# Order of the MLP outputs, roots and loads at the start of the MLP in a fused attention and MLP kernel

## The chip, the cores and the metric

The kernel runs on one core of a Trainium2 chip. The metric is the device time of one execution in microseconds, smaller is better; the time before is the median of four runs. Five engines work side by side, each through its own list of instructions in the order in which the program wrote them: TensorE (PE: matmuls, and PEld, the loading of weights), VectorE (DVE), ScalarE (ACT), GpSimd (POOL) and SyncE (SP), which here only issues transfers. POOL and, at the start, ACT issue transfers too. An instruction that waits holds back all that stands behind it on its engine.

## What is computed

Attention over 8 batches, 12 heads, 448 positions and 64 columns, with queries and keys normalized by their root mean square, then an MLP over all 3584 positions (768 columns, 2048 hidden).

```python
def rmsnorm(x, g):
    rms = np.sqrt(np.mean(x * x, axis=-1, keepdims=True) + 1e-06)
    return x / rms * g
q_n, k_n = (rmsnorm(q, g_q), rmsnorm(k, g_k))
scores = scale * np.matmul(q_n, k_n.transpose(0, 1, 3, 2))
...
attn = attn / (np.sum(attn, axis=-1, keepdims=True) + 1e-09)
return np.matmul(attn, v).astype(np.float32)
...
x = np.ascontiguousarray(attn_out.transpose(0, 2, 1, 3)).reshape(B * S, H * D)
...
h = x @ w_in
g = np.maximum(h, 0.0) + alpha * np.minimum(h, 0.0)
return (g @ w_out).astype(np.float32)
```

## The kernel before

**Groups.** A batch is cut into three groups of four heads, so there are 24 groups; group `y` belongs to batch `y // 3`. For q and for k of a group, these steps run one after the other:

- `load_qk` (line 97): two transfers each for q and k from HBM into a tile `nat`, four in all, issued by SP. There are six `nat` tiles, so group `y` uses those of group `y - 3`, and can be loaded when that one has been scaled.
- `square` (141): POOL squares `nat` into `sq` (ACT does so for groups 0 and 1). `reduce` (151): VectorE sums the squares over 64 columns into `ss`.
- `root` (159): ACT computes the inverse root by a logarithm and an exponential, for q and k together. `scale` (168): POOL multiplies (`qs`), but for four tiles that VectorE takes.
- The turn to columns-first: groups 0 to 5 are turned on TensorE (`turn`, 188, tiles `tps`). From group 6 on, `turn_dma` (178) lets SP issue two transposing transfers, `qT` and `kT`, as soon as `scale` is done, and `turn` then only has VectorE multiply `kT` by the gain (line 192).

**Attention of a group.** `score` (225) makes one of seven tiles of scores in PSUM (`sc`, two tiles of two banks), `soft` (243) takes the exponential on ACT. `den` (269) sums the exponentials by matmul, `log` and `invert` (276, 281) make the inverse on ACT, `attv` (285) multiplies with the values (`load_v`, 111, issued by POOL) and VectorE writes `xT` (lines 310 and 312).

**MLP.** `up(b, ft)` (344) makes 128 of the 2048 hidden columns of a batch, here called unit `ft`: six matmuls into a PSUM tile, then ACT makes `ah`, which is alpha times that, and VectorE the maximum of both, `gT`. `down` (357) multiplies with `w_out`, VectorE copies the result to `osb` (line 377), and SP issues two stores. The jobs that `down` is handed (reduces of later groups) go ahead of the copy on VectorE, and a `turn` behind it. The PSUM tiles for MLP results are two of one bank each (tag "mm"), and now and then the two-bank tile of tag "acc", which `den` and `attv` use as well. For batch 0, units 0 to 3 begin before the last group of the batch is done (`begin`, 335), and units 2 and 3 share the two banks of one "acc" tile, `hTb`.

**Weights.** `load_w_in` and `load_w_out` (119, 131) are issued by POOL, a quarter at a time. The first half of an output takes quarters 0 and 1 of `w_out`, the second half quarters 2 and 3.

**Order.** The work is put in 69 steps called bursts, each with up to four score tiles. Lines 402 to 485 work out in which burst each step stands: `den_at`, `av_at`, `turn_at`, and from them `prep` (ahead of a burst's scores), `post` (behind all its work), `roots` and `jobs` (steps that go one by one behind the MLP units of the burst). `gaps` holds the MLP units of each burst. A list `late` holds steps that wait until so many units are done. Worked out for the bursts in question:

| burst | score tiles (group, tile) | attention | MLP | other steps |
|---|---|---|---|---|
| 10 | (3,0) (3,1) (3,2) | sums and values of group 2 | units 0 to 4 of batch 0 | root and scale of 4, reduces of 5; behind it, quarters 0 and 1 of `w_out`, squares of 6 |
| 11 | (3,3) (3,4) | | units 5, 6 | root and scale of 5 |
| 12 | (3,5) (3,6) | | units 7, 8 | loads of 7, values of batch 1, turn of 4, quarter 2 of `w_out` |
| 13 | (4,0) (4,1) | | units 9 to 11 | reduces of 6 |
| 14 | (4,2) (4,3) | | units 12, 13 | root, scale and transposes of 6, squares of 7, quarter 3 of `w_out` |
| 15 | (4,4) (4,5) | | units 14, 15 | loads of 8, turn of 5 |
| 16 | (4,6) (5,0) | | one `down` | loads of 9, reduces of 7 |
| 17 | (5,1) (5,2) (5,3) | sums of 3 and 4 | one `down` | root, scale and transposes of 7, turn of 6, squares of 8 |
| 18 | (5,4) (5,5) (5,6) (6,0) | values of 3 and 4 | one `down` | squares of 9 |
| 19 | (6,1) (6,2) (6,3) | sums of 5 | one `down` (second half) | loads of 10, reduces of 8, turn of 7 |
| 20 | (6,4) (6,5) (6,6) | values of 5 | one `down` (second half) | values of batch 2, root, scale and transposes of 8, reduces of 9 |
| 21 | (7,0) (7,1) | | units 0 to 3 of batch 1 | root, scale and transposes of 9 |

Burst 10 is the one that the code calls `lead`: its root and scales wait in `late` until four units are done, and its jobs begin behind the fourth unit (line 704).

Of the kernel before, what the change touches and what calls it, by code (L numbers as in the profile page):

```python
# [10 lines left out]
FP16 = mybir.dt.float16  # L11
AF = mybir.ActivationFunctionType
# [9 lines left out]
def kernel(  # L22
# [12 lines left out]
    nc = tc.nc  # L35

    B, H, S, D = q.shape
# [4 lines left out]
    G = HH // 2  # L42
# [14 lines left out]
    ffn = ctx.enter_context(tc.tile_pool(name="ffn", bufs=2))  # L57
# [26 lines left out]
    alpha_sb = cols[:, :NF]  # L84
# [3 lines left out]
    gT = cst.tile([128, NF, W], FP16, name="gT", tag="gT")  # L88
# [180 lines left out]
    def den(ys):  # L269
        dn = psa.tile([128, 2, 512], FP32, name="dn", tag="acc")  # L270
        over_keys(
            (dn[:, 0], dn[:, 1]), ys, lambda g, y, par, c, j: ones[ds(64 * g, 64), c]
        )
        rden[ys] = dn
# [40 lines left out]
    def bank(name, spare):  # L315
        if spare:
            t = psa.tile([128, 2, 512], FP32, name=name + "a", tag="acc")
            return t[:, 0]
        return psf.tile([128, 512], FP32, name=name, tag="mm")
# [3 lines left out]
    def up_part(hT, b, ft, lo, hi):  # L323

        for i in range(lo, hi):
            for g in range(2):
                nc.tensor.matmul(  # L327
                    out=hT[:, :S],
                    lhsT=w_in_sb[:, g * G + i, ts(ft, 128)],
                    rhs=xT[b][:, g, i, :],  # L330
                    start=(i == 0 and g == 0),
                    stop=(i == G - 1 and g == 1),
                )

    def begin(ft):

        if ft < 2:
            begun[ft] = bank("hT", False)
        elif ft == 2:
            t = psa.tile([128, 2, 512], FP32, name="hTb", tag="acc")  # L340
            begun[2], begun[3] = t[:, 0], t[:, 1]
        up_part(begun[ft], 0, ft, 0, G - 1)

    def up(b, ft, spare=False):
        if b == 0 and ft in begun:
            hT = begun[ft]

            for n in {2: (2, 3), 3: ()}.get(ft, (ft,)):
                up_part(begun[n], 0, n, G - 1, G)
        else:  # L350
            hT = bank("hT", spare)
            up_part(hT, b, ft, 0, G)
        ah = ffn.tile([128, S], FP16, name="ah", tag="ah", bufs=3)
        nc.scalar.activation(out=ah, in_=hT[:, :S], func=AF.Copy, scale=alpha_sb[:, ft : ft + 1])  # L354
        nc.vector.tensor_max(out=gT[:, ft, ds((b & 1) * S, S)], in0=hT[:, :S], in1=ah)  # L355

    def down(b0, t, oh, jobs=(), spare=False):

# [44 lines left out]
    den_at, av_at, split = {}, {}, {}  # L403
# [5 lines left out]
    while m < NG * J or steps:  # L409
        n = len(bursts)  # L410
        while steps:
# [14 lines left out]
        late = both or n in dens and n in avs or any(  # L426
            y >= G for y in dens.get(n, avs.get(n, ()))
        )
        limit = 2 + late + (both and avs[n][0] >= G)
        bursts.append([])  # L430
        while len(bursts[n]) < limit and m < NG * J:
            y, j = divmod(m, J)
# [13 lines left out]
    def at(n, f, *a):  # L446
        prep.setdefault(max(int(n), 0), []).append((f, a))

    def after(n, f, *a):
        post.setdefault(max(int(n), 0), []).append((f, a))  # L450
# [8 lines left out]
    jobs = {}  # L459
    for y in range(G, NG):  # L460

        early = y < G + 2
        if early:
            n = turn_at[y - 1] + 1
        elif y == G + 2:
            n = den_at[G - 1]
        elif y == 2 * G:
            n = turn_at[y] - 4
        elif y % G == 1:
            n = den_at[y - 4] - 1  # L470
        elif y % G:
            n = den_at[y - G]
        else:
            n = av_at[y - 4]
        at(n - (6 if early else 4 if y <= 3 * G else 5), load_qk, y)
        for nm in "qk":
            if y != 2 * G:
                after(n - 2, square, y, nm)
            if early:
                after(n, reduce, y, nm)  # L480
            else:
                jobs.setdefault(n, []).append((reduce, (y, nm)))
        roots[n + 1] = y
    for b in range(1, B):
        at(av_at[G * b] - 6, load_v, b)
# [82 lines left out]
    for n, g in enumerate((g_q, g_k)):  # L568
        for h in range(2):
            nc.gpsimd.dma_start(  # L570
                out=rows[NF + n : NF + n + 1, ds(64 * h, 64)], in_=g.unsqueeze(0)
# [13 lines left out]
    for nm in "qk":  # L585
# [3 lines left out]
        out=gain, in0=cols[:, NF : NF + 1], in1=cols[:, NF + 1 : NF + 2]  # L589
# [25 lines left out]
    for n in range(NB):  # L615
        for f, a in prep.get(n, ()):
            f(*a)
        tiles = bursts[n]

        lead = n == den_at[G - 1]  # L620
        first_tiles = tiles[: 2 if lead else split.get(n, 2)]
        for t in first_tiles:
            score(*t)
            if n == den_at[G - 1] - 1 and t == tiles[-1]:
                begin(0)
                begin(1)
            elif lead and t == tiles[0]:
                soft(*t)
                den(dens[n])
                attv(avs[n], 0, True, (log, invert))  # L630
            elif lead and t == tiles[1]:
                begin(2)
        plain = lead or n not in dens and n not in avs
        wait = plain and not lead and gaps[n] and gaps[n][0][0] is up
        if lead:
            begin(3)
        for t in tiles[:1] if wait else tiles[1:2] if lead else first_tiles:
            soft(*t)
        if n in dens and not lead:
            den(dens[n])  # L640
        if n in avs and not lead:

            for half in (1, 0) if avs[n] == (0, 1) else (0,):
                attv(avs[n], half)
        for t in () if lead else tiles[len(first_tiles) : 3]:
            score(*t)
            soft(*t)
        if n in avs and len(avs[n]) == 2 and avs[n] != (0, 1):
            attv(avs[n], 1)
        for t in () if lead else tiles[max(len(first_tiles), 3) :]:  # L650
            score(*t)
            soft(*t)
        late = []
        if wait:
            late = [(1, soft, t) for t in tiles[1:]]
        if n in roots:
            y = roots[n]
            work = [(root, (y,)), (scale, (y, "q")), (scale, (y, "k"))]
            if lead:

                late = [(2, score, tiles[2]), (2, soft, tiles[2])]
            if lead or wait and y < TD:
                late += [(4 if lead else 1, f, a) for f, a in work]
            else:
                for f, a in work:
                    f(*a)
            if y >= TD:
                turn_dma(y)
        if n in dens and not lead:
            log(dens[n])  # L670
            if gaps[n] and gaps[n][0][0] is down:
                invert(dens[n])
            else:
                late = [(1, invert, (dens[n],))]
        done = 0

        spare_at, clock = [], 0.0
        taken = n + 1 in dens or n + 1 in avs or turns.get(n + 1, TD) < TD
        for k, (f, a) in enumerate(gaps[n]):
            free = 2.3 if n in dens else (0.1, 1.2, 0.0)[len(avs.get(n, ()))]  # L680
            since += 1
            if clock >= free and not turns.get(n, TD) < TD and (
                since > 2 and not (taken and k == len(gaps[n]) - 1) or free == 0.0 and k == 0
            ):
                spare_at.append(k)
                since = 0
            clock += DOWN if f is down else UP
        ups_first = gaps[n] and gaps[n][0][0] is up
        if ups_first and n in dens and not lead:
            for f, a in jobs.pop(n, ()):  # L690
                f(*a)
        turned = n in turns and gaps[n] and (turns[n] >= TD or turns[n] < 2 * G)
        if turned and not ups_first and turns[n] >= TD:
            jobs.setdefault(n, []).append((turn, (turns[n],)))
        elif turned:
            turn(turns[n])
        for k, (f, a) in enumerate(gaps[n]):
            spare = k in spare_at
            if f is down:
                down(*a, jobs.pop(n, ()), spare)  # L700
            else:
                f(*a, spare)
                done += 1
                if n in jobs and not (lead and done < 4):
                    g, c = jobs[n].pop(0)
                    g(*c)
                    if not jobs[n]:
                        del jobs[n]
                while late and done == late[0][0]:
                    _, g, c = late.pop(0)  # L710
                    g(*c)
        if not gaps[n] and n in turns:
            turn(turns[n])
        for _, g, c in late:
            g(*c)
        if n < den_at[G - 1] - 1 and plain and n not in turns:
            spin(1)
        for f, a in jobs.pop(n, []) + post.get(n, []):
            f(*a)
# [32 lines left out]
```

## Time and profile before

| what | us |
|---|---|
| median of 4 runs | 432.69 |
| lowest and highest of them | 432.17, 434.82 |
| profiled execution, whole | 434.8 |
| profiled execution, span | 433.0 |
| TensorE busy in the span | 416.0 |
| idle time of TensorE up to 96 us, and from there on | 12.7, 4.4 |

The profile was taken in one execution with a span of 433.0 us; all times of instructions are in us from the start of that span. The page has the busy time of each engine, the span in 40 slices, the transfers, the chain of work that ended last, and the costliest groups of instructions. Behind it stand views of the same trace: the waits (who waited for whom: total, times, longest), the timeline of an engine (start, length, engine, line, operation, what it writes and reads, how many, and in brackets the idle time before it and what ended it), and the transfers. L355 is line 355 of the code before. Ends of matmuls are modelled, so neighbouring matmuls overlap by some 0.1 us in the timeline.

The granted TensorE clock is 1.00 throughout. The 16 transfer engines are busy for nearly the whole of the first 95 us (8 or 9 tenths in most of those slices) and 0.45 of the time after 140 us.

Units of burst 10 to 12 by the timelines: the matmuls of unit 4 start at 44.77, those of unit 5 at 46.51, of unit 6 at 49.56, of units 7 and 8 at 52.08. The scores of burst 13 start at 54.44, those of burst 17 at 69.60, of burst 21 at 93.56, and the first unit of batch 1 at 94.06.

### The profile page before, as it was taken

How to read it: one execution, taken by the hardware profiler on the slowest of the kernel's cores; microseconds unless marked ns; L12 is line 12 of the kernel's file. 1: busy time of each engine (PE TensorE's matmuls, PEld its weight loads, DVE VectorE, ACT ScalarE, POOL GpSimd, SP SyncE). 2: the span in 40 equal slices, each digit the busy share in tenths (PEclk: the TensorE clock that was granted, in tenths of full speed). 3: DMA queues.
4: the chain of work that ended last, by engine and by line, in shares of the span. 5: the costliest groups of instructions: out<-in, count | busy, mean ns of one | idle time of the engine just before them, and what ended most of it. 6: DMA issues, size and time to landing. Idle time of an engine off the chain costs nothing.

```text
span 433.0 us, 11487 instructions
## 1 busy us (share of the span) xinstructions
PE 416.0 (96%) x4964; PEld 215.9 (50%) x4964; DVE 203.4 (47%) x304; ACT 278.6 (64%) x385; POOL 175.2 (40%) x133
## 2 busy tenths in 40 slices
PE   7789899899999999999999999999999999999996
PEld 3344344444455445544555445554555445555554
DVE  2755664355555363545454463555453353233421
ACT  4997888668876577758757577757757577132300
POOL 4799696384093506380183606471063000000000
PEclk9999999999999999999999999999999999999999
DMA  8999899999759743788059842775074300211133
GB/s 188 232 226 216 149 213 152 224 190 192 169 98 193 166 104 62 156 154 189 21 87 193 170 130 55 147 153 123 20 121 84 77 1 21 56 38 31 25 73 75
DMA packets 70388, 53.85 MB, mean 124 GB/s; under 512 B 37425, under 2 KB 70337, under 8 KB 70337
## 3 DMA queue, kind: packets, MB, share of 16 engines
q1 hardware_dynamic: 55536, 40.19, 43.2%
q0 software_dynamic: 13984, 11.81, 18.9%
q10 hardware_dynamic: 816, 1.11, 1.1%
q8 instruction: 39, 0.64, 0.6%
q14 instruction: 13, 0.10, 0.1%
HBM read 45.62 MB, written 11.01 MB: 131 GB/s over the span
## 4 chain that ended last, share of the span: by engine, by line
PE 83%; DMA 6%; ACT 5%; DVE 4%; issue 1%; POOL 1%; SPq 0%; ACTq 0%
PE op L365 27%; PE hT L327 21%; PE hTa L327 10%; PE sc L232 7%; PE opa L365 6%; DMA w_out_sb<-in_moe_w_out_dram 4%; PE av L261 4%; PE dn L261 4%; ACT expT L246 3%; PE avb L261 2%; DMA nat<-in_k_dram 1%; DVE ss L154 1%; PE tps L206 1%; DVE gT L355 1%; POOL sq L148 1%
## 5 line engine op out<-in xcount | busy, mean ns | idle before, releaser
L246 ACT ACTIVATE expT<-sc,expb 128x896 f16<-128x896 f32 x168 | 161.4, 1003 | 37.9 <-PE sc L232 37.0
L171 POOL TENSOR_TENSOR qs<-nat,rr 128x896 f16<-128x896 f32 x44 | 76.7, 1762 | 149.4 <-issue 79.0
L365 PE MATMUL op<-w_out_sb,gT 128*128 128x384 f16 (+1 forms) x752 | 126.5, 323 | 1.1 <-DMA w_out_sb<-in_moe_w_out_dram 1.1
L365 PEld LDWEIGHTS <-gT 128*128 128x128 f16 x912 | 85.8, 98 | 66.7 <-issue 14.1
L327 PEld LDWEIGHTS <-w_in_sb 128*128 128x128 f16 x768 | 73.2, 98 | 75.9 <-issue 11.6
L327 PE MATMUL hT<-xT,w_in_sb 128*128 128x448 f16 x510 | 107.1, 353 | 2.9 <-DVE gT L355 2.2
L354 ACT ACTIVATE ah<-hT,cols 128x448 f16<-128x448 f32 x85 | 53.7, 633 | 44.6 <-PE hT L327 44.6
L148 POOL TENSOR_TENSOR sq<-nat 128x896 f32<-128x896 f32 x44 | 72.9, 1677 | 9.7 <-DMA nat<-in_q_dram 5.0
L355 DVE TENSOR_TENSOR gT<-hT,ah 128x448 f16<-128x448 f32 x85 | 52.8, 623 | 50.6 <-ACT ah L354 50.6
L377 DVE COPY osb<-op 128x384 f32<-128x384 f32 (+1 forms) x47 | 25.8, 548 | 86.7 <-PE op L365 86.7
L232 PE MATMUL sc<-qT,kT 64*32 64x448 f16 (+1 forms) x1092 | 53.2, 356 | 4.7 <-ACT expT L246 2.8
L154 DVE TENSOR_REDUCE ss<-sq 128x14 f32<-128x896 f32 x48 | 50.5, 1077 | 10.1 <-ACT sq L146 6.3
L327 PE MATMUL hTa<-xT,w_in_sb 128*128 128x448 f16 x246 | 53.2, 353 | 0.0
L354 ACT ACTIVATE ah<-hTa,cols 128x448 f16<-128x448 f32 x41 | 26.0, 634 | 31.4 <-PE hTa L327 31.4
L355 DVE TENSOR_TENSOR gT<-hTa,ah 128x448 f16<-128x448 f32 x41 | 25.6, 623 | 26.0 <-ACT ah L354 26.0
L232 PEld LDWEIGHTS <-kT 64*32 64x32 f16 (+1 forms) x1092 | 15.0, 93 | 36.7 <-issue 30.4
L365 PE MATMUL opa<-w_out_sb,gT 128*128 128x384 f16 x160 | 27.7, 327 | 0.6 <-DVE xT L312 0.6
L312 DVE TENSOR_TENSOR xT<-av,rden 128x896 f16<-128x896 f32 x16 | 17.4, 1090 | 18.0 <-PE av L261 14.1
L261 PEld LDWEIGHTS <-vt 64*32 64x32 f16 (+1 forms) x1260 | 18.9, 94 | 13.2 <-issue 2.2
L261 PE MATMUL dn<-expT,ones 64*32 64x448 f16 (+1 forms) x812 | 24.2, 350 | 0.9
L261 PE MATMUL av<-expT,vt 64*32 64x448 f16 (+1 forms) x812 | 24.1, 350 | 0.0
L278 ACT ACTIVATE rden<-dn 128x896 f32<-128x896 f32 x16 | 14.5, 907 | 7.3 <-PE dn L261 7.3
(45 smaller groups left out, 158.9 us busy)
## 6 DMA issues: line engine op xcount, KB each, us to landing
out_dram<-osb SPq DMA_DIRECT2D x109, 96.0 KB, 2.3
nat<-in_q_dram SPq DMA_DIRECT2D x46, 224.0 KB, 5.2
nat<-in_k_dram SPq DMA_DIRECT2D x46, 224.0 KB, 6.9
vt<-in_v_dram POOLq DMA_DIRECT2D x16, 336.0 KB, 6.8
w_in_sb<-in_moe_w_in_dram POOLq DMA_DIRECT2D x12, 256.0 KB, 7.9
w_out_sb<-in_moe_w_out_dram POOLq DMA_DIRECT2D x4, 768.0 KB, 12.5
nat<-in_q_dram ACTq DMA_DIRECT2D x2, 224.0 KB, 4.7
nat<-in_k_dram ACTq DMA_DIRECT2D x2, 224.0 KB, 6.6
```

What stands on the lines that cost most here:

```text
L148: nc.gpsimd.tensor_mul(out=sqf, in0=src, in1=src)
L154: nc.vector.tensor_reduce(out=ss_t[y][:, "qk".index(nm)].rearrange("p h j -> p (h j)").unsqueeze(2), in_=sqs[y, nm], axis=AXIS_X, op=ALU.add,)
L171: eng.tensor_mul(out=t.rearrange("p j h d -> p h j d"), in0=nat[y, nm], in1=rr_t[y][:, "qk".index(nm)].unsqueeze(3).broadcast_to((128, 2, ...
L232: nc.tensor.matmul(out=sc[ds(64 * g + m * c, m), par, :S].rearrange("p (j c) -> p j c", j=J), lhsT=kT[ds(64 * par, 64), j, g, ts(c, m)], r ...
L246: nc.scalar.activation(out=expT[y][:, j], in_=scs[y, j][:, :, :S], func=AF.Exp, scale=QK_SCALE, bias=expb[:, 0:1],)
L261: nc.tensor.matmul(out=accs[g][ds(m * h, m), :S], lhsT=weights(g, y, par, ts(c, m), j), rhs=expT[y][ds(64 * g, 64), j, par, :], start=(j = ...
L312: nc.vector.tensor_mul(out=x, in0=av[:, :, :S], in1=r)
L327: nc.tensor.matmul(out=hT[:, :S], lhsT=w_in_sb[:, g * G + i, ts(ft, 128)], rhs=xT[b][:, g, i, :], start=(i == 0 and g == 0), stop=(i == G ...
L354: nc.scalar.activation(out=ah, in_=hT[:, :S], func=AF.Copy, scale=alpha_sb[:, ft : ft + 1])
L355: nc.vector.tensor_max(out=gT[:, ft, ds((b & 1) * S, S)], in0=hT[:, :S], in1=ah)
L365: nc.tensor.matmul(out=ops[c][:, :PW], lhsT=gT[:, ft, ts(t, 128)], rhs=w_out_sb[:, ft, ds(oh * OH + c * PW, PW)], start=(ft == 0), stop=(f ...
L377: nc.vector.tensor_copy(out=o[:, ts(c, PW)], in_=ops[c][:, :PW])
```

## The change

It has four parts, all of them about the order in which the same instructions are written out.

- The output of units 2 and 3 of batch 0 (ah on ACT, the maximum on VectorE) is held back until unit 4's has been written: first unit 4's ah and maximum, then ah of 2 and of 3, then the maxima of 2 and of 3. `prelu` does this for a list of units, all ah first.
- In burst 10, root and scales of group 4 wait for two units instead of four, so they stand behind the exponential of tile (3,2) and ahead of all these outputs. The jobs of the burst begin behind the fifth unit instead of the fourth.
- The reduce of k of group 5 moves from burst 10 to burst 11, where it stands behind the output of unit 5. Root 5 follows in burst 11, as before.
- The loads of groups 8 and 9 move from ahead of bursts 15 and 16 to behind the work of burst 17, so that SP meets them behind the transposes of group 7 and the stores of bursts 16 and 17. Those of group 8 stand just ahead of its squares.

```diff
--- before.py
+++ after.py
@@ -341,6 +341,20 @@
             begun[2], begun[3] = t[:, 0], t[:, 1]
         up_part(begun[ft], 0, ft, 0, G - 1)
 
+    held = []
+
+    def prelu(units, b):
+
+        ahs = []
+        for hT, ft in units:
+            ah = ffn.tile([128, S], FP16, name="ah", tag="ah", bufs=3)
+            nc.scalar.activation(
+                out=ah, in_=hT[:, :S], func=AF.Copy, scale=alpha_sb[:, ft : ft + 1]
+            )
+            ahs.append(ah)
+        for (hT, ft), ah in zip(units, ahs):
+            nc.vector.tensor_max(out=gT[:, ft, ds((b & 1) * S, S)], in0=hT[:, :S], in1=ah)
+
     def up(b, ft, spare=False):
         if b == 0 and ft in begun:
             hT = begun[ft]
@@ -350,9 +364,14 @@
         else:
             hT = bank("hT", spare)
             up_part(hT, b, ft, 0, G)
-        ah = ffn.tile([128, S], FP16, name="ah", tag="ah", bufs=3)
-        nc.scalar.activation(out=ah, in_=hT[:, :S], func=AF.Copy, scale=alpha_sb[:, ft : ft + 1])
-        nc.vector.tensor_max(out=gT[:, ft, ds((b & 1) * S, S)], in0=hT[:, :S], in1=ah)
+        if b == 0 and ft in (2, 3):
+            held.append((hT, ft))
+            return
+        units = [(hT, ft)]
+        if b == 0 and ft == 4:
+            prelu(units, b)
+            units = held
+        prelu(units, b)
 
     def down(b0, t, oh, jobs=(), spare=False):
 
@@ -472,14 +491,18 @@
             n = den_at[y - G]
         else:
             n = av_at[y - 4]
-        at(n - (6 if early else 4 if y <= 3 * G else 5), load_qk, y)
+        if y in (2 * G + 2, 3 * G):
+
+            after(den_at[G], load_qk, y)
+        else:
+            at(n - (6 if early else 4 if y <= 3 * G else 5), load_qk, y)
         for nm in "qk":
             if y != 2 * G:
                 after(n - 2, square, y, nm)
             if early:
                 after(n, reduce, y, nm)
             else:
-                jobs.setdefault(n, []).append((reduce, (y, nm)))
+                jobs.setdefault(n + (y == G + 2 and nm == "k"), []).append((reduce, (y, nm)))
         roots[n + 1] = y
     for b in range(1, B):
         at(av_at[G * b] - 6, load_v, b)
@@ -660,7 +683,7 @@
 
                 late = [(2, score, tiles[2]), (2, soft, tiles[2])]
             if lead or wait and y < TD:
-                late += [(4 if lead else 1, f, a) for f, a in work]
+                late += [(2 if lead else 1, f, a) for f, a in work]
             else:
                 for f, a in work:
                     f(*a)
@@ -701,7 +724,7 @@
             else:
                 f(*a, spare)
                 done += 1
-                if n in jobs and not (lead and done < 4):
+                if n in jobs and not (lead and done < 5):
                     g, c = jobs[n].pop(0)
                     g(*c)
                     if not jobs[n]:
```

## Prediction

> **What bounds the kernel now.** I read the page first: TensorE is busy 416.0 of 433.0 us at a granted clock of 1.00 in every slice, so its own matmuls set the time and only its idle 17 us can be won. Then the waits of PE. From 96 us to the end that list is empty; all named waits lie before.
>
> ```profile
> PE 416.0 (96%) x4964; PEld 215.9 (50%) x4964; DVE 203.4 (47%) x304; ACT 278.6 (64%) x385; POOL 175.2 (40%) x133
> PE sc L232 <- ACT expT L246: 2.8, 7, 0.6
> PE hT L327 <- DVE gT L355: 2.2, 2, 1.7
> PE op L365 <- DMA w_out_sb<-in_moe_w_out_dram: 1.1, 1, 1.1
> PE opa L365 <- DVE xT L312: 0.6, 1, 0.6
> PE sc L232 <- DVE kT L192: 0.5, 1, 0.5
> ```
>
> The columns are total, times, longest. Third, the timelines (start and length in us; VectorE, then ScalarE) around the 1.7 us wait: unit 6's matmul at 49.56 needs the bank of unit 4.
>
> ```profile
> 46.03 0.62 DVE L355 TENSOR_TENSOR gT<-hTb,ah 128x448 f16<-128x448 f32 x1 [0.79 <-ACT ah L354]
> 47.90 1.08 DVE L154 TENSOR_REDUCE ss<-sq 128x14 f32<-128x896 f32 x1
> 48.89 0.62 DVE L355 TENSOR_TENSOR gT<-hT,ah 128x448 f16<-128x448 f32 x1
> 46.69 0.63 ACT L354 ACTIVATE ah<-hTb,cols 128x448 f16<-128x448 f32 x1 [0.69 <-DVE gT L355]
> 47.69 0.62 ACT L354 ACTIVATE ah<-hT,cols 128x448 f16<-128x448 f32 x1
> ```
>
> Unit 4's matmuls end at 46.08, but its ah runs only at 47.69, behind unit 3's (which waits for unit 2's output of the same PSUM tile) and a root; its output then stands behind a reduce. Fourth, the chain of waits, and the queue of SP with POOL's squares of groups 8 and 9:
>
> ```profile
> 65.17 3.21 POOL sq L148 x2
> 68.38 19.03 DMA w_out_sb<-in_moe_w_out_dram
> 87.45 1.46 PE op L365 x8
> 74.19 4.70 SPq L105 DMA_DIRECT2D nat<-in_k_dram  x2
> 83.86 1.25 SPq L181 DMA_TRANSPOSE qT<-qs  x1
> 85.24 3.66 SPq L181 DMA_TRANSPOSE kT<-qs  x1
> 85.33 1.68 POOL L148 TENSOR_TENSOR sq<-nat 128x896 f32<-128x896 f32 x1 [2.28 <-DMA nat<-in_k_dram]
> 88.14 3.32 POOL L148 TENSOR_TENSOR sq<-nat 128x896 f32<-128x896 f32 x2 [1.13 <-DVE ss L154]
> 91.68 0.63 DVE L192 TENSOR_SCALAR kT<-kT,gain 128x896 f16<-128x896 f16 x1 [2.17 <-DMA kT<-qs]
> ```
>
> The last weight quarter takes 19.03 us to land, while the eight loads of groups 8 and 9 (69.29 to 78.89) run beside it; the transposes of group 7, whose source was scaled by 76.93, are issued only at 83.86, behind those loads. From 77 to 85 us the SP queue moved 1.38 MB and POOL's 0.59 MB: the loads took most of the bandwidth.
>
> **Part 1: order of the outputs and roots (bursts 10 to 12).** No instruction is added or removed. ACT (steps from the trace: exponential to the next 0.89, ah 0.52, root pair 0.49): exponential 44.47, root of group 4 45.36 instead of 47.22, ah 4 at 46.10 as its matmuls end, ah 2 46.62, ah 3 47.14, exponential 47.66, ah 5 48.55, exponential 49.07, free at 49.96. VectorE: output of 4 at 46.76 to 47.38, so unit 6 starts at 47.7 as PE reaches it: the 1.74 us wait goes. What is late next: the outputs of 2 and 3. Does unit 2's output wait for ah 3, which reads the other bank of the tile? The row above says yes, since ah 3 waited 0.69 us for unit 2's output there. So 47.80 and 48.34, the reduce of q at 48.88, output 5 at 49.87, the reduce of k at 50.41 to 51.49. Root 5 comes behind that on ACT, before ah 6, and holds it until 51.52 (before: 50.53). Then ah 6 at 52.01, exponential 52.53, ah 7 53.42, exponential 53.94, ah 8 54.83. Before, these last three stood at 53.42, 53.95 and 54.84. ACT is back where it was; unit 8 can start at 53.33, when output 6 frees its bank, ends at 54.6, and the scores that follow at 54.44 lose 0.1. I take **0** for PE, with 0 - 0.2 and + 0.4 as ends (the latter if output 2 doesn't wait for ah 3: everything behind it about 0.45 earlier).
>
> The Trainium skill, "PSUM — Partial Sum Buffer", section "PSUM bank collisions raise a hardware error", asks for guarding by bank and quadrant only, since engines on different banks ran clean there. By it output 2 would need no wait for ah 3, and the part would be worth the 0.4 of the upper end; the trace's 0.69 us wait between two banks of one tile decides for 0.
>
> Off the path, the root's 1.86 us reach POOL: scales of group 4 at 45.95 to 49.27 instead of 47.88 to 51.21. Behind them stand the first two weight quarters (51.16 to 49.3), the squares of 6, the scales of 5, the values of batch 1 and the third quarter (60.89 to 59.1). The scales of 6 keep to their root (61.05, 0.8 earlier), and so the last quarter goes out at 67.6 instead of 68.38. SP issues loads of group 7 1.9 us earlier for the same reason.
>
> **Part 2: loads of 8 and 9 behind turn 7.** Eight issues of some 0.62 us leave SP's queue between transposes 6 and the first output stores, and stand behind transposes 7 and the stores of burst 17.
>
> Gains. (a) Transposes 6 land at 78.27 in the trace, under the third and fourth quarter. Those come earlier, so I let kT 6 land by 75 to 77; then VectorE scales it and takes the values at 76.65 when av ends, not at 78.66: 0.45 and 0.61 go, **1.06**. Its cover is the av matmuls to 76.59; if it lands at 78 again, nothing is won here. (b) The last quarter has the 8 us in which it got 0.59 of 1.97 MB to itself, and is there by 80, while PE wants it at 86.3 - 1.06 = 85.2: **1.13** go. Sum on PE: **2.2** at burst 20.
>
> Costs. First issue of load 8, called L. Root 7 ends at 73.46 as before, scales 7 at 76.93 on POOL, kT 7 is issued at 76.98. Its issue takes 1.2 (the shortest rows) to 3.66 (the row above), 2.39 in the row at 121.73, which had empty queues; I take 1.9. Two stores of 0.6 each follow: L = 78.98 + 1.2, about 80.1, bounds 79.4 and 81.8. Eight loads in a row landed, in the trace at 106.61 (a queue as free), 4.6, 6.75, 8.65 and 10.2 us behind the first issue, pair by pair. So squares of 8 on POOL at L + 4.75 and L + 6.9, of 9 at L + 8.8 and L + 10.45 (1.68 each). VectorE: reduce 8 k to L + 9.7, the output copy of burst 19 0.5, kT 7 0.45, the last values 1.05, reduces of 9 to L + 13.65. Behind them on ACT root 9, and on VectorE the copy that frees a bank for unit 2 of batch 1. In the trace the reduce ends at 95.28. So this chain gains 95.28 - 13.65 - L = **81.6 - L**: 1.5 at 80.1, 2.2 at 79.4, a loss of 0.2 at 81.8. All behind waits for the smaller of it and PE's 2.2; the copy's bank allows some 0.3 more than root 9. Two stages later (ah 0 at 94.3, output 2 of batch 1 ends at 97.5, unit 4 at 97.55 instead of 99.21) PE is **1.65** ahead.
>
> Other things moved: load 10 and stores 18 stand behind load 9 (issued till 85.3) and still go before 91.50, so load 10 isn't late. The values load of batch 2 and scales 8 move on POOL from 92.77 to 93.5; transposes 8 follow within 0.3 of before with fewer loads beside them, and are needed at 103.6 (now 105.52, landing 105.50); if they keep that landing, VectorE is held 1.9 us with slack of about as much. From 99 us PE is full and keeps what it has.
>
> The Trainium skill, "DMA: Bandwidth & Descriptors", section "Rules for kernel authors", speaks against this part: issue a DMA early and wait late. Followed, the loads would stay, and the 1.06 and 1.13 would remain lost; the 19.03 us landing shows here what an early load costs its neighbours.
>
> **Sum.** 433.0 - 1.65 = 431.35 for the span; the profiled execution took 434.8, 1.8 around the span, which is 2.1 above the median 432.69. For the median: 432.69 - 1.65 = **431.0**. About 0.5% (2.2 us) is what a measurement of this kernel can tell from no change.
>
> **Rivals.** *Everything goes (0.25):* output 2 is free of ah 3 and kT 7 issues in 1.2, so PE's 2.2 + 0.4 decide: 430.1. For it the short issues from 136 us on; against it the 0.69 wait. *The transfers were hidden anyway (0.15):* kT 6 lands at 78 again, and L is 81: 0.6, 432.1. For it transposes' slow 10.6 and 13.1 us under load; against it the quarters that come earlier. *Loads too late (0.12), the slower side:* place, POOL's square of 9 k and behind it reduce and root 9; price 1 us for each us of L beyond 81.6. If kT 7's issue takes 3.66 and its landing holds load 9 (in the trace a DMA of SP goes out when the one eight before has landed, as at 78.29 behind 78.27), L is worth 84: 435.1. For it, the loads lose up to 11 us of lead and POOL waits 4.4 us for them even now; against it, no other load is in flight by then. *Forecast (0.48):* 431.0, own range 430.5 to 431.8.
>
> **Range and chances.** 429.9 to 433.3: the first rival and 0.2 below it, the second whole, of the third what L up to 82.2 gives. Faster by over 0.5% (under 430.5): the first rival and a little of the forecast, 0.28. Slower by over 0.5%: most of the third and what I overlooked, 0.11. Between: 0.61.
>
> **What would show it.** Right: no wait for gT near 49 us, yet ACT at an exponential near 53.9; a root on ACT waiting 1 us or more for a reduce near 51; no PE wait for w_out nor for kT 6; first load 8 near 80, root 9 near 93.8. Wrong: unit 9's matmuls well before 55.0; load 8 issued after 81.6; a wait of PE for the copy or for gT between 90 and 97; transposes 8 landing after 104.

## The result, and the profile after

The changed kernel takes 434.13 us (median of 42 executions, 432.79 to 437.32), the kernel before 432.88 (median of 61, 431.19 to 438.28). The ratio is 1.0035, with a 95% interval of 1.002 to 1.0049: 0.9 to 2.1 us slower. The prediction had 431.0. The loss is there as well among executions whose granted clock stood at 0.998 or more: on the chip of b1_after these have a mean of 433.66 for the kernel before (22 executions) and of 435.03 for the changed one (10).

The profiled execution of the changed kernel took 434.16, close to its median. Its span is 432.4, and it reaches the first score of burst 10 at 36.89 where the one before did so at 38.01. So it is 1.12 us ahead before anything that was changed, and its times below are to be read with 1.12 added when they are held against those of the prediction. The waits of PE in the changed kernel (total, times, longest):

```profile
PE sc L232 <- ACT expT L246: 3.6, 7, 0.9
PE sc L232 <- DVE kT L192: 1.8, 1, 1.8
PE hT L327 <- DVE gT L356: 1.3, 3, 0.8
PE hT L327 <- DVE osb L396: 0.5, 1, 0.5
```

The wait of 1.7 for gT has become three short ones, and those for `w_out` and for `xT` are gone. New is one of 1.8 us for kT: the first score of group 7 at burst 21. The chain of waits (start, length, what) says where it comes from:

```profile
81.18 6.48 DMA nat<-in_k_dram
...
87.81 1.69 POOL sq L148
...
89.53 0.04 DVE ss L154
89.56 0.96 issue
90.53 0.55 DVE osb L396
91.08 0.76 DVE kT L192
91.83 1.00 DVE xT L312
...
93.75 1.08 DVE ss L154
...
94.85 0.33 ACT rr L165
```

The second transfer for k of group 8 lands at 87.65; its square, its reduce, the copy of burst 19 and only then kT of group 7 follow, one behind the other. (What the chain calls "issue" at 89.56 is the rest of that reduce, which runs to 90.62.) The transposed kT itself had been in place since 81.39. The row of the scaling on VectorE, and SP's queue ahead of the first load:

```profile
90.99 0.84 DVE L192 TENSOR_SCALAR kT<-kT,gain 128x896 f16<-128x896 f16 x1
75.84 1.23 SPq L181 DMA_TRANSPOSE kT<-qs  x1
77.17 1.91 SPq L404 DMA_DIRECT2D out_dram<-osb  x2
79.12 1.36 SPq L105 DMA_DIRECT2D nat<-in_q_dram  x2
```

ScalarE around burst 10, and behind it two waits of PE:

```profile
45.52 1.15 ACT L351 ACTIVATE ah<-hTb,cols 128x448 f16<-128x448 f32 x2
50.41 0.32 ACT L165 ACTIVATE rr<-ss,epsb 128x28 f32<-128x28 f32 x1 [1.42 <-DVE ss L154]
53.71 0.65 ACT L351 ACTIVATE ah<-hT,cols 128x448 f16<-128x448 f32 x1
49.05 0.38 PE L232 MATMUL sc<-qT,kT 64*64 64x448 f16 x4 [0.90 <-ACT expT L246]
52.22 1.29 PE L327 MATMUL hT<-xT,w_in_sb 128*128 128x448 f16 x6 [0.77 <-DVE gT L356]
```

The two ah of the shared tile now run in one go, the root of group 5 waits 1.42 us for the reduce that was moved, and ah 8 stands at 53.71, which is 54.83 by the clock of before. PE, free of unit 6's wait, now waits 0.90 us for an exponential and 0.77 us for the bank of unit 8.

What bursts cost is read best from the starts of their first scores on PE. The table has the time from the start of one burst to that of another, in us, for every profiled execution of this study; the last column is the whole execution.

| kernel | 10-13 | 13-18 | 18 | 19 | 20 | 21 | 22-23 | 10-24 | whole |
|---|---|---|---|---|---|---|---|---|---|
| before, first profile | 16.44 | 20.12 | 7.92 | 6.35 | 4.72 | 5.15 | 10.30 | 71.00 | 434.8 |
| before, b1_before | 16.44 | 20.12 | 6.73 | 6.08 | 4.72 | 5.32 | 10.51 | 69.91 | 432.64 |
| before, d1_before_3 | 16.45 | 20.14 | 8.64 | 9.24 | 5.20 | 5.15 | 10.30 | 75.12 | 437.79 |
| changed, first profile | 16.56 | 20.01 | 6.73 | 5.06 | 6.64 | 6.00 | 10.51 | 71.50 | 434.16 |
| changed, b1_after | 16.56 | 20.00 | 6.73 | 5.06 | 6.93 | 6.83 | 10.30 | 72.42 | 435.49 |
| b1_part1 | 16.56 | 20.00 | 7.97 | 6.56 | 4.72 | 5.15 | 10.30 | 71.26 | 434.45 |
| b1_part2 | 16.44 | 20.12 | 7.93 | 5.06 | 7.57 | 6.00 | 10.51 | 73.62 | 436.97 |
| c1_ahead | 16.55 | 20.00 | 6.73 | 5.06 | 4.72 | 5.15 | 10.44 | 68.66 | 431.79 |
| d1_ahead_2 | 16.57 | 20.02 | 7.05 | 5.06 | 5.24 | 7.49 | 10.51 | 71.95 | 434.48 |
| d1_ahead_3 | 16.56 | 20.00 | 7.61 | 5.06 | 5.16 | 7.48 | 10.51 | 72.39 | 435.1 |
| c1_load9 | 16.56 | 20.01 | 10.53 | 5.06 | 4.72 | 5.97 | 10.51 | 73.36 | 436.65 |
| c1_root5 | 15.63 | 20.24 | 7.56 | 7.91 | 6.29 | 5.15 | 10.30 | 73.08 | 436.07 |
| c1_both | 15.63 | 20.24 | 8.10 | 5.06 | 4.72 | 6.93 | 10.51 | 71.20 | 433.77 |
| d1_fetch | 16.55 | 20.01 | 6.73 | 5.06 | 4.72 | 5.71 | 10.51 | 69.29 | 435.35 |
| e1_w3 | 16.44 | 20.13 | 8.48 | 5.06 | 4.72 | 5.15 | 10.30 | 70.29 | 434.04 |
| e1_w3_part1 | 16.57 | 20.01 | 8.53 | 5.06 | 4.72 | 5.15 | 10.30 | 70.34 | 433.26 |
| e1_w3_root5 | 15.63 | 20.24 | 8.51 | 5.06 | 4.72 | 5.15 | 10.30 | 69.62 | 432.51 |

From burst 24 to the end every one of them takes 323.98 to 324.02 us. Without any wait the bursts take 6.73 (18), 5.06 (19), 4.72 (20) and 5.15 (21). The profile b1_before lies 0.24 us from the median of its kernel, the changed kernel's first profile 0.03 from its own, so these two are the typical pair: 69.91 against 71.50, and in it + 0.12 and - 0.11 from part 1, - 1.02 in burst 19, + 1.92 in burst 20, + 0.68 in burst 21. That sum, + 1.59, lies within the measured loss of 0.9 to 2.1.

Not all of the table is waits. In five of the profiles the granted TensorE clock stood at 0.50 for 3.41 us (twice in d1_fetch): from 88.98 in d1_before_3, 93.27 in b1_after, 77.69 in c1_load9, 88.31 in c1_root5, 17.94 and 24.77 in d1_fetch. In the first four this begins at the end of a wait of PE of 2.9, 2.1, 1.9 and 2.6 us, or up to 1.3 us behind it; a wait of 2.8 in b1_part2 and those of 1.9 to 2.0 in the changed kernel, d1_ahead_2 and d1_ahead_3 have none behind them. The same 56 matmuls in the changed kernel at full clock, and in c1_load9 during such a stretch:

```profile
75.72 1.52 PE L261 MATMUL avb<-expT,vt 64*32 64x448 f16 x56
79.14 2.46 PE L261 MATMUL avb<-expT,vt 64*32 64x448 f16 x56
```

So a long wait can cost another 1.7 us (an estimate, half of the 3.41), which the list of waits doesn't show. The typical pair has no such stretch.

### The profile page after: what moved, and what is told of

Same layout as the page of the kernel before. It is cut to its first block, busy times and chain, and to the rows that moved or that the text cites. A ratio compares the mean times of both kernels' runs of the same rounds, so it can differ in the third digit from the quotient of the medians.

```text
span 432.4 us, 11486 instructions
## 1 busy us (share of the span) xinstructions
PE 417.1 (96%) x4964; PEld 216.2 (50%) x4964; DVE 204.2 (47%) x304; ACT 279.0 (65%) x385; POOL 175.2 (41%) x133
## 4 chain that ended last, share of the span: by engine, by line
PE 80%; ACT 5%; DVE 5%; DMA 3%; issue 2%; POOL 2%; SPq 1%; POOLq 0%; DVEq 0%; ACTq 0%
PE op L384 26%; PE hT L327 21%; PE hTa L327 10%; PE sc L232 7%; PE opa L384 6%; PE dn L261 4%; PE av L261 4%; ACT expT L246 3%; DMA nat<-in_k_dram 3%; DVE ss L154 2%; PE avb L261 2%; DVE gT L356 1%; ACT ah L351 1%; DVE osb L396 1%; POOL qs L171 1%
## 5 line engine op out<-in xcount | busy, mean ns | idle before, releaser
L327 PEld LDWEIGHTS <-w_in_sb 128*128 128x128 f16 x768 | 73.2, 98 | 75.1 <-issue 10.8
```

The costliest lines, as they stand in the source:

```text
L327: nc.tensor.matmul(out=hT[:, :S], lhsT=w_in_sb[:, g * G + i, ts(ft, 128)], rhs=xT[b][:, g, i, :], start=(i == 0 and g == 0), stop=(i == G ...
```

## The experiments

**The two halves, and both kernels again.** Each half of the change alone; `b1_before` and `b1_after` are the two kernels without an edit.

```diff
 b1_part1: the changed kernel with
-        if y in (2 * G + 2, 3 * G):
-
-            after(den_at[G], load_qk, y)
-        else:
-            at(n - (6 if early else 4 if y <= 3 * G else 5), load_qk, y)
+        at(n - (6 if early else 4 if y <= 3 * G else 5), load_qk, y)
 b1_part2: the kernel before with the opposite edit
```

> The kernel before, unchanged, for a second profiled execution. If the first one was typical, the waits of PE for the last weight quarter (1.1) and for kT of group 6 with the values behind it (0.5 and 0.6) are there again, and unit 9's matmuls stand some 16.4 us behind the first score of burst 10. If that execution, whose 434.8 us lay 2 us above the median, was odd, these waits are smaller here, and what the change could win was smaller from the start.

> The change without its second part: outputs, roots and the reduce as in the changed kernel, loads of groups 8 and 9 where they were before. Theory A (the loads are the loss): the ratio to before is 1.000, within 0.001, since ACT waits for the reduce of k as long as it gains. Theory B (the held outputs and the early root are the loss): 1.002 to 1.004, the changed kernel's whole loss.

> The kernel before with the loads of groups 8 and 9 moved behind the work of burst 17, and nothing else. Theory A: 1.003 to 1.006, the whole loss or more, since the loads are issued here about as late but without the earlier scales of part 1; POOL then squares k of group 9 after 91 us and root 9 ends later than in the kernel before. Theory B: 1.000 or below.

> The changed kernel again, on the same chip as the two halves: 1.002 to 1.005. If the halves add up, its loss is the sum of theirs.

Measured ratios: part 1 0.9981 (0.9953 to 1.0009), part 2 1.0021 (0.9995 to 1.0047), both 1.0026 (1.0003 to 1.005). Part 1's interval leaves out the 1.002 to 1.004 of theory B (the outputs and the root are the loss); part 2's parts nothing, and the halves together would make 1.0002, which these intervals can't tell from 1.0026. The stretches show more. Part 1 costs 0.12 in bursts 10 to 12 and gets it back by 18, and the waits of the kernel before for the quarter and for kT 6 are all still there. Part 2 alone takes the wait in burst 19 away and puts 2.85 into burst 20 and 0.85 into burst 21. So the loads are the loss (theory A). The second profile of the kernel before has burst 18 without any wait, 1.2 us less than the first. Of its waits of PE:

```profile
PE hT L327 <- DVE gT L355: 2.3, 3, 1.7
...
PE op L365 <- DMA w_out_sb<-in_moe_w_out_dram: 0.9, 1, 0.9
```

In this list of PE's waits in b1_before, those for `xT` and for kT of 6 don't occur.

**Loads 2 us earlier, and loads of group 9 alone.**

```diff
 c1_ahead: the changed kernel, the loads in the main loop instead
-            after(den_at[G], load_qk, y)
+            pass
...
             if y >= TD:
                 turn_dma(y)
+            if y == 2 * G + 1:
+                load_qk(y + 1)
+                load_qk(y + 2)
 c1_load9: the changed kernel
-        if y in (2 * G + 2, 3 * G):
+        if y == 3 * G:
```

> The changed kernel with the loads of groups 8 and 9 issued right behind the transposes of group 7, ahead of the stores of burst 17: the first load goes out about 2.0 us earlier (near 77 in the clock of the changed kernel's profile). Theory A (the late loads set the end of bursts 20 to 22): each us of that comes back on TensorE, so its wait for kT of group 7 (1.8 to 2.1) and the copy's wait (0.5) go, bursts 10 to 24 take 70.0 to 70.6 instead of 71.5 and 72.4, and the ratio to before is 0.996 to 0.999. Rival (it is not the loads but the reduces' place on VectorE or the transfers as a whole): the wait stays above 1.5 and the ratio above 1.001.

> The changed kernel with the loads of group 8 back where they were before and only those of group 9 behind burst 17. Theory A: four loads beside the last weight quarter instead of eight, so the wait for it shrinks to 0 to 0.5, and group 9's loads land some 3 us earlier than in the changed kernel, being the first four of the row; no wait for kT of 7; bursts 10 to 24 take 69.8 to 70.5. Rival: the loads of 8 alone hold back transposes 6 and the quarter as much as all eight, and the waits of the kernel before (0.9 to 1.3) return.

The first profile of c1_ahead goes the way of theory A, and beyond the 70.0 to 70.6 that were expected: no wait in bursts 20 and 21, 68.66, the shortest of all. But its time is 1.002 of the kernel before (0.9992 to 1.0047), a miss. The profiled execution was the shortest of twelve (431.79, median 433.66), so two more executions were profiled.

> The kernel with the loads ahead of the stores, a second look. Its first profile was its fastest execution of twelve (431.79 against a median of 433.66). If the median has another cause than the loads, this execution shows where 1 to 2 us lie: the stretch of burst 18 (7.9 instead of 6.7, transposes 6 landing near 78), or a wait of PE that ends on nothing the profile shows.

> A third look at the same kernel, for the same question: how far the stretches of bursts 18 to 21 scatter between executions of one program.

Both have what the first lacked: 0.3 and 0.9 us in burst 18, and 2.3 in burst 21, where PE waits 2.0 for the copy that stands behind the reduces of group 9. The issue was earlier, by 1.2 and 1.9 us, but the landing was not: transposes 7, which are ahead of the loads in SP's queue, landed at 82.47 and 83.10 (81.39 in the changed kernel, 79.74 in the first profile), and the eighth load at 91.69 and 92.33 (91.31 in the changed kernel, 88.53 in the first profile). In these two of the three executions, sending the loads earlier gained nothing, since the transfers ahead of them landed later.

c1_load9 measured 1.0029 (1.0 to 1.0058). It has no wait for kT of 7 and none for the quarter, as theory A expects, but 3.8 us more in burst 18 and 0.8 more in burst 21, so its 73.36 misses the expectation. The loads of group 9 miss it too: SP issues them only at 85.99, behind transposes 7, of which the first took 5.13 us to issue and the second 4.18, and the last lands at 94.22 instead of some 3 us ahead of the changed kernel's 91.31. In burst 18, PE stood still in the middle of a run of matmuls:

```profile
77.75 0.94 PE L261 MATMUL av<-expT,vt 64*32 64x448 f16 x15 [1.92 <-issue]
```

Nothing in the program ends that wait. A 16 KB packet of the instruction queue, under way from 73.17, took 3.06 us then. Behind the first 14 us, nine of the 17 profiles have a wait of PE of this kind ("issue", 0.3 us or more), and all nine stand ahead of one of two places in PE's list: the 351st matmul in six, the 734th in three (0.32 in c1_root5, 0.53 in d1_ahead_3, 1.92 here). d1_fetch, described below, has 50 more matmuls ahead of this point, and its wait of 1.76 still stands ahead of the 351st, which there belongs to another step. In all nine PE goes on 1.4 to 1.8 us behind the end of the last instruction packet. So the place in the list counts and not the step, as it would if PE had run out of fetched instructions. Behind the wait the clock stands at 0.50 (above), which by estimate, half of 3.41, is worth 1.7 of the 3.8 us.

**What holds the fourth load.** In both profiles of the changed kernel the loads land 0.6 to 1.2 us apart, but the fourth 2.4 us behind the third (85.24 and 87.65; 85.86 and 88.29). At 84.0 and at 84.7 a packet of 16 KB on the instruction queue occupies one of the 16 transfer engines for 1.33 us. This is the queues' part of the transfer view of the changed kernel from 84 to 85.3 us (queue, kind, packets, MB, share):

```profile
q1 hardware_dynamic: 180, 0.27, 102.1%
q8 instruction: 1, 0.02, 6.4%
```

(6.4% of 16 engines over 1.3 us are the 1.33 us of the one packet.)

The page counts 39 such packets, 0.64 MB in all, which is 64 bytes for each of PE's 9928 matmuls and weight loads; so they are taken to be the fetch of PE's instructions, which the waits at fixed places in the list bear out. To move them, the five warm-up matmuls of bursts 0 to 6 became twelve small ones each, whose results nobody reads (the trace counts 50 more matmuls and 50 more weight loads):

```diff
-            spin(1)
+            fill(12)
...
+    def fill(count):
+
+        ps = psf.tile([128, 512], FP32, name="spin", tag="mm")
+        for _ in range(count):
+            nc.tensor.matmul(
+                out=ps[:, :64], lhsT=ident, rhs=idle[:, :64], start=True, stop=True
+            )
```

> The changed kernel with the five warm-up matmuls of bursts 0 to 6 replaced by twelve small ones each, which puts some 110 more instructions ahead in PE's list and nothing else behind. Theory F (the 16 KB packet of PE's instruction fetch, seen at 84.0 and 84.7 in the two profiles of the changed kernel, holds one of the 16 transfer engines, and every load behind it lands some 1.4 us late): the packets move to about 79 to 80 and 91 to 92, before and behind the eight loads; the gap between the third and the fourth load of group 8 falls from 2.4 to about 1.0 us, the eighth lands 10.5 to 11 us after the first issue instead of 12.2, and the wait of PE at burst 21 falls from 1.9 - 2.2 to under 1. Rival (the gap comes from the load itself, its place in HBM or the transposes ahead of it): the gap stays at 2.4 between the same two loads.

The packets came at 81.8, ahead of the first load's data, and at 94.1, behind the eighth's landing; between 83 and 94 us the same view has no line of the instruction queue. The eight loads landed 0.9 to 1.1 us apart, the eighth 10.8 us after the first issue. POOL's squares of groups 8 and 9 in this kernel, each of which starts as its load lands:

```profile
87.08 1.68 POOL L148 TENSOR_TENSOR sq<-nat 128x896 f32<-128x896 f32 x1 [7.66 <-DMA nat<-in_q_dram]
89.13 1.68 POOL L148 TENSOR_TENSOR sq<-nat 128x896 f32<-128x896 f32 x1 [0.37 <-DMA nat<-in_k_dram]
91.09 1.68 POOL L148 TENSOR_TENSOR sq<-nat 128x896 f32<-128x896 f32 x1 [0.29 <-DMA nat<-in_q_dram]
92.95 1.68 POOL L148 TENSOR_TENSOR sq<-nat 128x896 f32<-128x896 f32 x1 [0.18 <-DMA nat<-in_k_dram]
```

and in the changed kernel:

```profile
84.23 1.68 POOL L148 TENSOR_TENSOR sq<-nat 128x896 f32<-128x896 f32 x1 [8.42 <-DMA nat<-in_q_dram]
87.81 1.68 POOL L148 TENSOR_TENSOR sq<-nat 128x896 f32<-128x896 f32 x1 [1.90 <-DMA nat<-in_k_dram]
89.90 3.46 POOL L148 TENSOR_TENSOR sq<-nat 128x896 f32<-128x896 f32 x2 [0.41 <-DMA nat<-in_q_dram]
```

From q to k of group 8 it is 2.05 us instead of 3.58, and PE's wait at burst 21 is gone: bursts 10 to 24 take 69.29, 2.2 us less than in the changed kernel. Theory F holds, in one execution. Not all of the 2.2 us is the landing pace: the fourth load landed 2.1 us earlier, counted from the first score of burst 10, of which 1.55 are the pace and 0.53 an earlier issue. (The whole execution isn't shorter. It is 3.7 us late at burst 9: 1.6 by burst 8, with the two stretches of half clock, and 1.8 in the wait ahead of the 351st matmul.) In all seven profiles in which the eight loads come late and a packet falls among them, the jump follows the packet, wherever it falls, with 1.9 to 2.5 us for 0.6 to 1.3 between all other loads: between the second and third load in b1_part2, the third and fourth in the changed kernel, the fifth and sixth in c1_ahead, d1_ahead_2, d1_ahead_3 and c1_both. Where loads go out beside the last quarter, the landings are less even: 2.2 to 3.0 us behind the packet in the kernel before, b1_part1, c1_load9 and c1_root5, with up to 2.0 elsewhere, and only 1.4 to 1.7 behind it in the three e1 kernels below.

**A third execution of the kernel before.**

> A third execution of the kernel before. Theory A': the first profile (434.8) had an accident of its own in burst 18 (7.92 for 6.73) that the prediction counted as winnable; a typical execution has 6.73 there, and the wait for the last weight quarter of about 1.0 as the only sizable one behind burst 13.

A miss: 437.79, with 8.64 in burst 18 and a wait of 2.9 for the quarter. So what bursts 18 to 20 of this one kernel lose reaches from 1.0 to 6.6 us between executions (of the 6.6, some 1.7 are the stretch of half clock behind the wait for the quarter), and one profile is no measure of it. Transposes 6 land at 78.27, 74.88 and 77.91 in its three profiles, 40.3, 37.9 and 41.0 us behind the first score of burst 10.

**Root 5 one burst later, alone and with the loads ahead.**

```diff
 c1_root5: b1_part1 with
-        roots[n + 1] = y
+        roots[n + 1 + (y == G + 2)] = y
 c1_both: c1_ahead with the same edit
```

> Part 1 alone, with root and scales of group 5 one burst later. If the root that waits 1.4 us on ACT for the reduce of k is what takes back unit 6's 1.7 us, the stretch from burst 10 to burst 13 falls from 16.55 to between 15.4 and 15.9. If the held outputs or the scores' wait for exponentials take it back, it stays at 16.4 to 16.6. The whole time is expected at the kernel before's, since the waits for the last weight quarter come later.

> The changed kernel with loads 8 and 9 right behind transposes 7, and root 5 one burst later. Theory A: the two gains add as far as the loads' chain allows, bursts 10 to 24 in 69.2 to 70.2, ratio 0.994 to 0.998, the fastest of all so far. Rival: root 5's gain is lost again in front of the loads' chain, and it equals the kernel with the loads ahead alone.

Bursts 10 to 12 fall to 15.63, inside the expected range: the root that waits on ACT took back 0.93 of unit 6's 1.74 us, and unit 8's wait of 0.77 is gone. The rest was taken back by the wait of the scores for an exponential, which stays at 0.90, so the second reading holds in part as well. Alone, the gain ends in a wait of 2.6 for the quarter and a stretch of half clock behind it (burst 20 takes 6.29). c1_both measured 1.004 (1.0016 to 1.0064), a miss: waits of 0.6 each for kT 6 and `xT`, and 1.4 for the copy behind the reduces of group 9.

**The quarter earlier, the loads where they were.**

```diff
 e1_w3: the kernel before; e1_w3_part1: b1_part1; e1_w3_root5: c1_root5; each with
     for c in range(4):
         after(first + (0, 0, 2, 4)[c], load_w_out, c)
+    post[first + 4].insert(0, post[first + 4].pop())
```

> The kernel before with the last quarter of w_out issued ahead of the squares of group 7 instead of behind them, near 65.2 instead of 68.4. Reading one: the quarter lands 2 to 3 us earlier, its wait (0.9 to 1.1, up to 2.9) shrinks to 0 to 0.8, the loads of 8 and 9 and transposes 7 behind them land at most 0.5 us later, since the same bytes end at the same time; ratio 0.996 to 0.999. Reading two: the loads get less of the queue, land 2 us or more later, and the waits come back at bursts 20 and 21; ratio 1.000 to 1.003.

> Part 1 of the change, loads where they were before, last quarter ahead of the squares of group 7. Part 1 alone measured 0.998 (0.995 to 1.001) with a wait of 1.3 for the quarter. Reading one: that wait shrinks to 0 to 0.8, ratio 0.995 to 0.998. Reading two: 1.000 and above.

> The same with root 5 one burst later, which brought burst 13 forward by 0.9 us and then lost it in a wait of 2.6 for the quarter. With the quarter 3 us earlier the wait falls to about 1, and some 0.5 of the 0.9 is kept: ratio 0.994 to 0.998. If the queue sets the end of burst 20 whatever PE does, it equals the kernel with part 1 and the early quarter.

| kernel | median | ratio to before | interval |
|---|---|---|---|
| e1_w3 | 433.55 | 1.0 | 0.9972 to 1.0027 |
| e1_w3_part1 | 433.38 | 0.9974 | 0.995 to 0.9999 |
| e1_w3_root5 | 432.43 | 0.9963 | 0.9935 to 0.9991 |
| before, same chip | 433.65 | | |

In all three the quarter's wait is gone, as with the late loads, and bursts 20 and 21 have none: the eighth load lands at 87.35, 86.75 and 85.97, counted from the first score of burst 10 at most 0.3 us later than in the typical execution of the kernel before, and earlier than in its other two (89.04, 86.30, 89.01 by their own clocks). That is reading one. e1_w3 by itself misses its expected ratio, e1_w3_part1 and e1_w3_root5 meet theirs. In all three profiles kT of group 6 is waited for, some 1.0 us, and burst 18 takes 8.5, for 7.9 and 8.6 in the two slower executions of the kernel before; whether the earlier quarter causes that stays open. The waits of e1_w3_root5 from 40 to 100 us:

```profile
PE sc L232 <- ACT expT L246: 1.3, 3, 0.9
PE sc L232 <- DVE kT L192: 1.0, 1, 1.0
PE opa L384 <- DVE xT L312: 0.6, 1, 0.6
PE hT L327 <- DVE gT L356: 0.5, 1, 0.5
```

It keeps part 1 of the change, moves root 5 out of the way and wins the quarter's wait without touching the loads. It is faster than the kernel before, 0.9963, by 0.4 to 2.8 us, and so than the changed one, though it did not run beside that.

## Why the prediction was wrong

**Part 1 was right, term by term.** 0 was taken, with - 0.2 and + 0.4 as ends; the stretches show a loss of 0.12 that is back by burst 18. The output of unit 2 did wait for ah 3 (46.71, behind the pair of ah that ends at 46.67), so the wait between two banks of one tile held and the rule by banks did not decide. Unit 8 was put at 53.33 and starts at 53.34, ah 8 was put at 54.83 and stands there. The scales of group 4 came at 46.03 (45.95 predicted), the last quarter went out at 67.79 (67.6), all with the 1.12 added.

**The gains of part 2.** (b) was right: the quarter's wait is gone, 1.0 in the typical pair. (a), 1.06, was right for the execution that was read, and not for the kernel: transposes 6 did land at 75.95 (75 to 77 predicted), but in b1_before they do so at 75.93 by the same clock (74.88 and 1.05) with no change at all. The sum took the waits of one execution as the kernel's, though it lay 2.1 above the median, which the prediction itself noted.

**The cost of part 2 is the step that failed.** L was predicted at 80.1 and came at 80.24, in part by luck: the issue of kT 7 took 1.23 us where 1.9 were put, the two stores behind it 2.05 where 1.2 were. (In the working, 76.98 and 1.9 make 78.88, not 78.98; that changes nothing.) "Eight loads in a row landed, in the trace at 106.61 (a queue as free), 4.6, 6.75, 8.65 and 10.2 us behind the first issue" is wrong for this place: they landed 4.95, 8.53, 10.62 and 12.19 us behind it. No packet of the instruction queue falls among the landings that were taken as a model, until the last; here one does, and d1_fetch, without it, gives 4.93, 6.98, 8.95 and 10.80. So the reduces of group 9 ended at L + 15.7 instead of L + 13.65, and the chain, written as 81.6 - L, is 79.6 - L: a loss of 0.6 by the same row, where a gain of 1.5 was taken. Measured, root 9 stands at 95.97 for 95.32 before. In the typical execution of the kernel before, the reduces of group 9 end at 94.35 by the same clock (93.30 and 1.05), in the changed one at 95.93: 1.58 later, which is the loss of 1.59. The sum had no term for PE's wait at burst 21, now 1.85 us. The reduce of k of group 8 was put at L + 9.7 and ended at L + 11.5, 1.8 later, as its load did; the copy and the scaling of kT 7 behind it took 1.2 instead of 0.95 (the scaling 0.84 instead of 0.45).

**The sum.** Predicted for bursts 10 to 24: 71.00 - 1.65 = 69.35. Measured: 71.50. The landing explains most of these 2.15 us: d1_fetch, the same kernel without the packet, takes 69.29, with 0.5 us of that from an earlier issue. Held against the typical execution, a gain of 1.65 became a loss of 1.59; of these 3.24 us the other 1.09 are the point of comparison, 71.00 for a typical 69.91. In d1_fetch the change is worth 0.6 us against that execution.

**The rivals.** The slower one had place and mechanism right: square, reduce and root of the late loads. Its point was wrong: with the landings as they are, it decides from L = 79.6, not 81.6, and no late kT 7 was needed for it. c1_ahead shows that an earlier L alone isn't the cure: in two of its three profiles transposes 7 in front of the loads landed later and the loads with them. c1_ahead and the e1 kernels fit a simple reading, which no run isolates: the queue stays full until quarter, transposes and loads are through, and an order mostly chooses what ends last. In the kernel before that is transposes 7, with 0.5 us of VectorE behind them; in the changed one it is loads 8 and 9, with a square, a reduce, a copy and a root behind them, some 5 us.

## What to carry to other kernels

Price a moved load to the end of the work that it feeds, not to its issue. In a stretch where the transfer queues are full, it seems best to put last what has the least work behind it; that is argued from the chains here, not tested by itself. A landing pace is a row of its own place: look at what else runs on the transfer engines there, instruction fetches too. Before a wait is counted as winnable, see whether a second execution has it. And look at the granted clock behind a long wait before all of a longer stretch is called waiting.

## What the runs showed of the hardware that was not expected

Between 40 and 120 us, a 16 KB packet of the instruction queue took 0.9 to 1.4 us, and up to 3.1 us beside transposes. With the eight loads late, a load behind such a packet landed 1.9 to 2.5 us after the one before it in seven profiles, for 0.6 to 1.3 between all others, and in d1_fetch, where no packet fell among them, for 0.9 to 1.1. In the changed kernel the fourth, sixth and eighth load landed 1.4 to 1.7 us later behind the first issue than in d1_fetch. That part of a load waits behind the packet on one transfer engine is the reading; the trace doesn't show which engine moves what. The packets can be moved by adding instructions elsewhere in PE's list (50 matmuls and 50 weight loads brought those at 77.7 and 84.0 to 77.1 and 81.8, while PE itself ran 3.4 us later, and the next from 100.5 to 94.1).

PE's own waits that nothing in the program ends stood at the same two places in its list in nine profiles, 1.4 to 1.8 us behind the end of a packet. Behind waits of 1.9 to 2.9 us the granted clock was 0.50 for 3.41 us in four profiles, and behind others as long it was not. And in these 17 profiles the scatter lies ahead of burst 24: behind it, 324 us repeat within 0.04.
